# Scores of two head pairs at once on 64x64 tiles, and q and k side by side in 64 rows each

## The chip, the cores and the metric

The kernel runs on one core of a Trainium2 chip. TensorE (PE) multiplies matrices, VectorE (DVE), ScalarE (ACT) and GpSimd (POOL) work on their results, and DMA queues, issued by POOL and SyncE (SP), move data. The metric is the device time of one execution in microseconds (us); lower is better.

## The reference, cut to what matters

Eight batches of eight heads, 576 positions, 64 numbers a head. Attention in a window of 32 positions to either side, plus 8 global positions that see all and are seen by all; then a two-layer network with softplus over the 4608 tokens.

```python
scores = (1 / sqrt(64)) * q @ k.T                       # B=8, H=8, S=576, D=64
mask = |i - j| <= 32  or  i is global  or  j is global  # 8 global positions
attn = softmax(where(mask, scores, -1e9)) @ v
x = attn.transpose(0, 2, 1, 3).reshape(4608, 512)
h = x @ w_in                                            # 512 -> 2048
out = softplus(h) @ w_out                               # 2048 -> 512
```

## The kernel before

**Units.** A unit is 64 query positions of one batch, all eight heads: 9 units a batch, 72 in all. The heads go in four pairs p; a pair's two heads h lie one above the other in 64 rows each. A unit's keys are 136 columns: 64 + 64 of the window and 8 global ones.

**From q and k to scores.** `load_qk` brings q or k of a batch into `qn` or `kn`: 72 rows, each with 8 successive positions of all heads. `tk` and `tq` (L533, L544) turn them, 16 transposes of 72x64 for a pair of heads; `kev` and `qev` copy the results to `kx` and `qx` (copies show as L448). For batches after the first, `qx` holds each unit's 64 queries of the two heads in separate halves of 128 columns, the rest zero (the zeros are set once, by `blanks_q`), so that one matmul of 128x128 with 136 columns gives both heads' scores (`sc`, L662): four matmuls a unit. For batch 0 the queries lie without zeros, and each head has a matmul of its own on a 64x64 tile (L667). `pick` (L491) multiplies with a 0/1 matrix and so gathers the 8 global rows of k and of q, eight matmuls of 512 columns each; `keep`, `turn`, `fill` and `gev` bring them into `kx` and `qg`.

**From scores to tokens.** `top` (L673, DVE) adds the mask and takes the greatest; `ex` (L694, ACT) the exponentials; `su` (L702 to L704, DVE) sums and their inverse; `no` and `gc` (L710, L714, POOL) multiply. The probabilities are turned by PE (`tp`, L720) or by a DMA (`pt`). `val` makes values for four units: 16 or 8 matmuls on 64x64 tiles for the global rows (L775), then 32 on 128x64 tiles for the windows (L785). The global queries have a chain of their own (`sg`, `mx`, `gexp`, `gsum`, `tg`, `lge`, `ov`, `oz`); L610 is in `gsum`.

**MoE.** Nine tiles of 512 tokens: `first` (L819, 64 matmuls of 512 columns), `soft` (L825, ACT), `second` (L830, 64 matmuls), `oev` and the store.

**The order.** Nothing runs in program order: each piece of work is a job with a cost on its engine, a rank, what it waits for and which buffers it opens, and `_Order.run` walks through them once, before the launch, and lays down the order of each engine. `KINDS` says for each kind of PSUM tile how many of the eight banks it may hold and how many must be left spare; `SLOTS` does the same for SBUF; `SWITCH` is what it counts for a change of TensorE's tile shape (`array`); `ASKS`, `HOLDS` and `COMES` are its model of the fetch of PE's instructions. `OPENING` and `LATER` add to the ranks. `add_scores` puts the scores of a tile's units between the `first` jobs of the tile before; `make_batch` adds the work on a new batch's q and k, behind the exponentials of the tile's last unit.

Of the kernel before, what the change touches and what calls it, by code (L numbers as in the profile page):

```python
# [18 lines left out]
class _Order:  # L19
# [30 lines left out]

    def closed(self, key):
        if key is None:
            return 0
        ends = [u["end"] for u in self.users[key]]
        return None if None in ends else max(ends) + self.HOP

    def room(self, opens):

        t0 = 0
        want = 0  # L60
        spare = 0
        for pool, key in opens:
            cap = self.slots.get(pool) or self.kinds[pool][0]
            was = self.opened[pool]
            if len(was) >= cap:
                t = self.closed(was[-cap])
# [12 lines left out]

    def run(self, free):  # L80
# [16 lines left out]
        while ready:  # L97
            best = None
            for j in ready:
# [8 lines left out]
                for e in j["cost"]:  # L108
                    t = max(t0, free[e])
                    rank = j["rank"]  # L110
                    if e == "PE" and array != 128:
                        rank = 0 if j["array"] == array else rank + 1
# [23 lines left out]
            if e == "PE" and j["array"] != array:  # L136
                array = j["array"]
                t += self.SWITCH
# [34 lines left out]
def kernel(  # L173
# [39 lines left out]
    HALVED = 1  # L213
    TURNED = 16
# [26 lines left out]

    def load_qk(b, which, h0=0, h1=H):
# [3 lines left out]
    Q_PARTS = ((0, 0, 32), (32, G, NQ - 32))  # L246
# [15 lines left out]
    load_qk(0, 1, H // 2, H)  # L262
# [25 lines left out]
    posQ2 = temp([P, QR], FP32, "posQ2")  # L288
    count(posQ2[0:G, :], [[1, QR]], 0, QR)
    count(posQ2[G:P, :], [[1, QR]], 32 * QR, QR)  # L290
    pick_w = const([P, QR, 32], BF16, "pick")
    pick_0 = const([P, QR, 32], BF16, "pick0")
# [7 lines left out]
    qx = [const([P, HP, NJ, 2, G], BF16, f"qx{i}") for i in range(2)]  # L300
# [8 lines left out]
    def blanks_q(i):  # L309
        def edges():  # L310
            nc.gpsimd.memset(kx[i][:, :, 0, 0:WIN].bitcast(I32), 0)
            nc.gpsimd.memset(kx[i][:, :, NH5 - 1, G - WIN:G].bitcast(I32), 0)
            clear(nc.gpsimd, qg[i][:])
        return [edges] + [lambda p=p, h=h: nc.gpsimd.memset(qx[i][h * D:(h + 1) * D, p, :, 1 - h, :].bitcast(I32), 0)
                          for p in range(HP) for h in range(2)]
# [13 lines left out]
    for lo, at, n in Q_PARTS:  # L329
        nc.gpsimd.dma_start(out=qn[at:at + n, :, :],  # L330
                            in_=q[0].rearrange("h (q r) d -> q h (r d)", r=QR)[lo:lo + n])
# [50 lines left out]
    def ones_g(i):  # L382
# [3 lines left out]
        for p in range(1, HP):  # L386
            nc.vector.tensor_copy(gw[i][:, :, p, 0:2 * NG], gw[i][:, :, 0, 0:2 * NG])
# [22 lines left out]
    ST, PEB, PNB, PTB, RB = 10, 5, 8, 12, 2  # L410
# [43 lines left out]
    def add_load(b, which, deps):  # L454
# [8 lines left out]
        if b:  # L463
            T["load", b, which] = [o.add({"POOL": (880, 0)}, lambda e: load_qk(b, which), deps + early, rank=0, moves=4300)]
# [9 lines left out]
    def add_prep(b, gate, rank):  # L474
# [4 lines left out]
        if b < 2:  # L479
            blanks["g"] = [T["edges", 0] if b == 0 else T["blank_q", 1]]  # L480
        XN = (qn, kn)

        def pick(e, w):
# [3 lines left out]
            parts = ((pick_w, 0, NQ),) if b or w else tuple((pick_0, at, n) for lo, at, n in Q_PARTS)  # L487
# [21 lines left out]
        def gev(e):  # L509
            for h in range(2):  # L510
                r = slice(h * D, (h + 1) * D)
                copy(e, qg[i][r, :, h * NG:(h + 1) * NG], PS["gt", b][r, 0, :, 0:NG])
        for n, w in enumerate((1, 0)):
            T["pick", b, n] = o.add({"PE": (460 * (1 if b or w else 2), 530 * (1 if b or w else 2))}, lambda e, w=w: pick(e, w),
# [6 lines left out]
                                    [T["keep", b, n], T.get(("turn", b, n - 1)), T["sel8"]], rank=4,  # L521
# [5 lines left out]
        plain = qx[0][:].rearrange("c p j h q -> c p (j h q)")[:, :, 0:S]  # L527
        for p in range(HP):
# [18 lines left out]

            def kev(e, p=p):
# [7 lines left out]
            def qev(e, z=0, p=p, parts=parts):  # L556
                lo, at, n = parts[z]
                t = PS["tq", b, p, z][:].rearrange("c r (j q) -> c j q r", q=G // QR)
                if b == 0:
                    copy(e, plain[:, p, lo * QR:(lo + n) * QR].rearrange("c (j q r) -> c j q r", q=G // QR, r=QR), t)  # L560
                    return
                for h in range(2):
                    c = slice(h * D, (h + 1) * D)
                    copy(e, qx[i][c, p, :, h, :].rearrange("c j (q r) -> c j q r", r=QR), t[c])
            T["tk", b, p] = o.add(mm(QR, NQ), tk, [T["load", b, 1][b == 0 and p >= HP // 2], *gate], rank=rank, opens=[("tk" if b else "tk0", ("tk", b, p))], array=64)
            T["kev", b, p] = o.add({"ACT": (635, 720), "DVE": (800, 880)}, kev, [T["tk", b, p], *late, *blanks["g"]],
                                   rank=3, uses=[("tk", b, p)])
            for z, (lo, at, n) in enumerate(parts):
                key = ("tq", b, p, z)
                T["tqb" if z else "tq", b, p] = o.add(mm(QR, n), lambda e, z=z, f=tq: f(e, z), [T["load", b, 0][z], *gate], rank=rank + z,  # L570
                                                      opens=[("tq" if b else "tq0", key)], array=64)
                n = QR * n
                T["qevb" if z else "qev", b, p] = o.add({"ACT": act(n), "DVE": (90 + 1.2 * n, 170 + 1.2 * n)} if b == 0 else {"ACT": (1270, 1370), "DVE": (1530, 1600)},
                                                        lambda e, z=z, f=qev: f(e, z), [T["tqb" if z else "tq", b, p], *late], rank=3 + z, uses=[key])

        if b == 0:
            T["pick", 0, 1]["deps"] += [T["tqb", 0, HP - 1], T["make_pick"]]
# [3 lines left out]
    def add_global(b, gate, early):  # L581
# [24 lines left out]
        def gsum(e):  # L606
# [3 lines left out]
            nc.vector.scalar_tensor_tensor(out=rv[i][:, 0:2], in0=selg[:, 0, :], scalar=rv[i][:, 2:3], in1=selg[:, 1, :],  # L610
                                           op0=OP.mult, op1=OP.add)
# [27 lines left out]
        T["gsum", b] = o.add({"DVE": (530, 630)}, gsum, [T["gexp", b], T["select"], T.get(("oz", b - 2))], rank=2)  # L639
# [9 lines left out]
    def add_scores(n, gate, rank):  # L649
# [3 lines left out]
        def sc(e, x):  # L653
            if x == 0:
                PS["st", n] = sb.tile([P, HP, EXT], FP32, tag="st", name="st", bufs=ST)
                PS["nb", n] = sb.tile([P, HP], FP32, tag="nb", name="nb", bufs=ST)
            kf = kx[i][:].rearrange("c p a w -> c p (a w)")
            ps = PS["s", n, x] = psum(("s", n, x), [P, 2, EXT], FP32)
            for y in range(2):
                p = x * 2 + y  # L660
                if b:
                    nc.tensor.matmul(out=ps[:, y, :], lhsT=qx[i][:, p, j, :, :].rearrange("c h q -> c (h q)"),  # L662
                                     rhs=kf[:, p, j * W:j * W + EXT], start=True, stop=True)
                    continue
                for h in range(2):
                    r = slice(h * D, (h + 1) * D)
                    nc.tensor.matmul(out=ps[r, y, :], lhsT=qx[0][:].rearrange("c p j h q -> c p (j h q)")[r, p, j * G:(j + 1) * G],  # L667
                                     rhs=kf[r, p, j * W:j * W + EXT], start=True, stop=True)

        def top(e, x):  # L670
            for y in range(2):
                p = x * 2 + y
                nc.vector.tensor_tensor_reduce(out=PS["st", n][:, p, :], in0=PS["s", n, x][:, y, :], in1=mask[:, j, :],  # L673
                                               scale=-SCALE, scalar=3.0e38, op0=OP.add, op1=OP.min,
                                               accum_out=PS["nb", n][:, p:p + 1])
        for x in range(2):
            ready = [T["kev", b, x * 2 + y] for y in range(2)] + [T["fill", b]]
            ready += [T["qevb" if b == 0 and j > 3 else "qev", b, x * 2 + y] for y in range(2)] + [T["blank_q", 2 - b] if 0 < b < 3 else None]
            T["sc", n, x] = o.add(mm(2 if b else 2, EXT), lambda e, x=x: sc(e, x), ready + gate, rank=rank, array=128 if b else 64,
                                  opens=[("s", ("s", n, x))] + ([("st", ("st", n))] if x == 0 else []))  # L680
            gate = [*gate, T["sc", n, 0]]
            T["top", n, x] = o.add({"DVE": (440, 600)}, lambda e, x=x: top(e, x), [T["sc", n, x], *T["mask", 0]], rank=3 if n < 8 else 4,
                                   uses=[("s", n, x), ("st", n)])
# [61 lines left out]
    def add_values(n4):  # L745
# [13 lines left out]
        def val(e):  # L759
# [9 lines left out]
            for y in range(2):  # L769
                for u, e_, b in spans:  # L770
                    for half in range(2):
                        k = slice(half * G, (half + 1) * G)
                        for c in range(2):
                            r = slice(c * G, (c + 1) * G)
                            nc.tensor.matmul(out=PS["xo", n4, half][r, y, u:e_, :], lhsT=oz[b % 2][k, y, r],  # L775
                                             rhs=PS["R", n4][k, u:e_, r], start=(y == 0 and u == 0), stop=False)
            for half in range(2):
                for y in range(2):
                    p = half * 2 + y
# [266 lines left out]
```

## Time and profile before

| | before |
|---|---|
| median of 3 runs | 372.12 us (370.07 to 372.55) |
| profiled execution | 371.55 us, its span 369.8 us |
| PE / DVE / ACT / POOL busy | 95% / 65% / 75% / 41% |
| scores after batch 0 (L662), 128x128, 136 columns | 252 matmuls |
| transposes of k and q (L533, L544) | 1088 matmuls |
| pick (L491) | 136 matmuls |
| first matmul of the MoE (L819) starts | 34.03 us |
| loads of q and k after batch 0 | 14 DMAs of 576 KB, 12.1 and 14.6 us to landing |

A profile page lists, of one execution, how busy each engine was, the chain of work that ended last followed back to the start, and groups of instructions by source line. The trace behind it answers for stages, single lines and stretches of time. The end of a matmul is modelled, so for PE the differences between starts are safer than the lengths shown.

### The profile page before, as it was taken

What the parts mean: (1) busy time and instruction counts of PE and PEld (TensorE: products, weight loads), DVE (VectorE), ACT (ScalarE), POOL (GpSimd) and SP (SyncE); (2) the same over time, 40 slices, a digit from 0 to 9 for tenths busy, and PEclk for the clock granted to TensorE, in tenths of its full rate; (3) what the DMA queues carried; (4) which work ended last, traced back from release to release, by engine and by line L of the source; (5) the groups of instructions that cost most, each with busy time, mean ns of one, the idle gap of its engine ahead of it and who ended that gap; (6) DMA issues with size and microseconds to landing.
All of it is one profiled execution on the core that took longest, in us unless ns stands there. A gap on an engine that the chain in (4) does not pass through costs nothing.

```text
span 369.8 us, 10736 instructions
## 1 busy us (share of the span) xinstructions
PE 350.3 (95%) x4044; PEld 194.3 (53%) x4044; DVE 239.5 (65%) x1028; ACT 277.2 (75%) x724; POOL 153.4 (41%) x258
## 2 busy tenths in 40 slices
PE   1977999999999999999999999999999999999996
PEld 0744777465545554555455545544554455445444
DVE  5689758996679756975697569755975595163011
ACT  3695898997599759885988598959895986784710
POOL 8988820691038503940295029502840180060000
PEclk9999999999999999999999999999999999999999
DMA  6999993099319981698159916980692022021002
GB/s 95 153 234 188 195 168 61 31 104 176 88 44 144 153 156 45 130 144 166 40 132 122 183 40 139 139 170 31 143 107 76 29 87 59 1 73 58 0 30 85
DMA packets 86164, 38.99 MB, mean 105 GB/s; under 512 B 68064, under 2 KB 79584, under 8 KB 86112
## 3 DMA queue, kind: packets, MB, share of 16 engines
q0 software_dynamic: 53248, 18.37, 46.8%
q1 hardware_dynamic: 32864, 19.94, 23.7%
q8 instruction: 31, 0.51, 0.6%
q14 instruction: 21, 0.17, 0.2%
HBM read 36.71 MB, written 9.44 MB: 125 GB/s over the span
## 4 chain that ended last, share of the span: by engine, by line
PE 68%; DVE 15%; ACT 7%; DMA 4%; issue 3%; POOL 3%; DVEq 0%; POOLq 0%; ACTq 0%
PE h L819 34%; PE o L830 16%; DVE sm L702 6%; PE s L662 4%; PE xo L785 3%; ACT pe L694 2%; PE tq L544 2%; DMA qn<-in_q_dram 2%; DVE rs L704 2%; PE pick L491 2%; DVE rs L703 2%; PE tk L533 2%; DVE osb L448 2%; PE xo L775 1%; ACT L602 1%
## 5 line engine op out<-in xcount | busy, mean ns | idle before, releaser
L710 POOL TENSOR_TENSOR pn<-pe,rs 128x512 bf16<-128x512 f32 x72 | 74.7, 1039 | 169.5 <-DVE rs L704 134.4
L819 PE MATMUL h<-xT,win 128*128 128x512 bf16 (+1 forms) x640 | 138.8, 361 | 0.1
L830 PE MATMUL o<-wout,g 128*128 128x512 bf16 (+1 forms) x592 | 136.2, 374 | 0.0
L825 ACT ACTIVATE g<-h 128x512 bf16<-128x512 f32 (+1 forms) x160 | 86.0, 558 | 41.9 <-PE h L819 40.9
L673 DVE CUSTOM_DVE_ANT_0 st<-s,mask 128x136 f32<-128x136 f32 x288 | 69.8, 295 | 45.3 <-PE s L662 43.8
L694 ACT ACTIVATE pe<-st,nb 128x136 f32<-128x136 f32 x288 | 92.1, 403 | 0.8 <-DVE nb L673 0.7
L819 PEld LDWEIGHTS <-win 128*128 128x128 bf16 x640 | 60.1, 99 | 50.9 <-issue 2.0
L830 PEld LDWEIGHTS <-g 128*128 128x128 bf16 x592 | 55.1, 98 | 57.2 <-issue 3.3
L702 DVE TENSOR_REDUCE sm<-pe 128x4 f32<-128x544 f32 x63 | 44.8, 711 | 10.0 <-ACT pe L694 9.8
L448 DVE COPY osb<-o 128x512 f32<-128x512 f32 (+1 forms) x26 | 17.3, 664 | 28.2 <-PE o L830 28.1
L251 POOL DMA_DIRECT2D vA<-in_v_dram x40 | 34.3, 874 | 0.0
L448 DVE COPY qx<-tq 64x576 bf16<-64x576 bf16 (+2 forms) x35 | 25.5, 728 | 5.6 <-PE tq L544 5.0
L662 PEld LDWEIGHTS <-qx 128*128 128x128 bf16 x252 | 20.5, 98 | 14.2 <-issue 0.3
L662 PE MATMUL s<-kx,qx 128*128 128x136 bf16 x252 | 26.9, 223 | 0.0
L673 DVE DVE_READ_ACCUMULATOR2_ANT nb<- 128x1 f32 x288 | 23.8, 83 | 0.0
L448 ACT CAST xT<-xo 128x512 bf16<-128x512 f32 x19 | 10.9, 590 | 12.1 <-PE xo L785 12.1
L533 PE MATMUL tk<-ident_b,kn 72*64 72x72 bf16 x512 | 13.5, 205 | 6.2 <-DMA kn<-in_k_dram 6.2
L448 ACT COPY kx<-tk 128x32 bf16<-128x32 bf16 (+1 forms) x75 | 18.0, 359 | 1.9 <-PE tk L533 1.8
L704 DVE TENSOR_TENSOR rs<-rs,notg 128x4 f32<-128x4 f32 x72 | 17.7, 246 | 2.5
L448 ACT COPY qx<-tq 64x576 bf16<-64x576 bf16 (+2 forms) x29 | 17.2, 593 | 1.9 <-PE tq L544 1.6
L714 POOL TENSOR_TENSOR gw<-pe,rs 128x32 bf16<-128x32 f32 x72 | 17.2, 238 | 3.0 <-DVE rs L704 1.8
L703 DVE RECIPROCAL rs<-sm 128x4 f32<-128x4 f32 x72 | 12.7, 177 | 6.5
(113 smaller groups left out, 347.5 us busy)
## 6 DMA issues: line engine op xcount, KB each, us to landing
out_dram<-osb SPq DMA_DIRECT2D x35, 256.0 KB, 2.2
vB<-vA SPq DMA_DIRECT2D x16, 256.0 KB, 7.0
kn<-in_k_dram POOLq DMA_DIRECT2D x7, 576.0 KB, 12.1
qn<-in_q_dram POOLq DMA_DIRECT2D x7, 576.0 KB, 14.6
vA<-in_v_dram POOLq DMA_DIRECT2D x24, 128.0 KB, 6.4
win<-in_moe_w_in_dram POOLq DMA_DIRECT2D x2, 1024.0 KB, 15.6
wout<-in_moe_w_out_dram POOLq DMA_DIRECT2D x4, 512.0 KB, 10.7
vA<-in_v_dram POOLq DMA_DIRECT2D x16, 96.0 KB, 5.2
```

What stands on the lines that cost most here:

```text
L251: nc.gpsimd.dma_start(out=vA[b % 2][p0:p0 + hi - lo, t, :].rearrange("p (h d) -> p h d", h=H), in_=SRC[2][b, :, lo:hi, :].rearrange("h s d ...
L448: (nc.scalar.copy if e == "ACT" else nc.vector.tensor_copy)(out, in_)
L533: nc.tensor.transpose(out=ps[h * D:(h + 1) * D, r, :], in_=kn[0:NQ, p * 2 + h, r * D:(r + 1) * D], identity=ident_b[0:NQ, 0:NQ])
L662: nc.tensor.matmul(out=ps[:, y, :], lhsT=qx[i][:, p, j, :, :].rearrange("c h q -> c (h q)"), rhs=kf[:, p, j * W:j * W + EXT], start=True, ...
L673: nc.vector.tensor_tensor_reduce(out=PS["st", n][:, p, :], in0=PS["s", n, x][:, y, :], in1=mask[:, j, :], scale=-SCALE, scalar=3.0e38, op0 ...
L694: nc.scalar.activation(out=pe[:, p, 0:EXT], in_=PS["st", n][:, p, :], func=AF.Exp, bias=PS["nb", n][:, p:p + 1], scale=-1.0, **({"accum_ou ...
L702: nc.vector.reduce_sum(out=sm[:], in_=PS["pe", n][:, :, 0:EXT], axis=AX)
L704: nc.vector.tensor_tensor(out=rs[:], in0=rs[:], in1=notg[:, j:j + 1].to_broadcast([P, HP]), op=OP.mult)
L710: nc.gpsimd.tensor_tensor(out=pn[:].rearrange("c p (a s) -> c p a s", a=2), in0=wide[:, :, :, 0:G], in1=rs[:].unsqueeze(2).unsqueeze(3).to ...
L819: nc.tensor.matmul(out=h[:, :], lhsT=w_in_t[c * P // WC][:, kd, c * P % WC:c * P % WC + P], rhs=PS["xT", m][:, kd, lo:hi], start=(kd == 0) ...
L825: nc.scalar.activation(out=PS["g", m, c][:, lo:hi], in_=PS[key][:, :], func=AF.Softplus)
L830: nc.tensor.matmul(out=PS[key][:, :], lhsT=PS["g", m, kf][:, ns * P:(ns + 1) * P], rhs=w_out_t[kf // 4][:, kf % 4, lo:hi], start=(kf == 0) ...
```

## The change

- **Scores.** `qx` has no zeros any more. A unit's scores are eight matmuls on 64x64 tiles. In pair y = 0 head h has rows and columns h; in pair y = 1 the column half is swapped (`h ^ y`), so that two pairs use all four 64x64 tiles. For batches after the first, three units make one job (a burst), in four PSUM banks, 24 matmuls.
- **What follows from the swap.** `ones_g` and `val` use `c ^ y` likewise; `gsum`'s scalar_tensor_tensor becomes two tensor_scalars. `val` may run its two parts in either order (`flip`), whichever meets the tile shape that PE is in.
- **q and k side by side (batches 1 to 7).** One tile `nq` holds q in rows 64 to 127 and k in rows 0 to 63: 8 successive positions a row for the first 512 positions, one a row for the last 64. Each load is two DMAs (`load_main`, `load_rest`). `tkq` turns both at once on 64x64 tiles, 36 transposes of 64 columns a pair of heads, two pairs a job; `kev2` and `qev2` copy. `pick_both` gathers from q and k together on 64x32 tiles, 16 matmuls of 512 columns and 8 of 128.
- **Batch 0.** Loads in the order k heads 0-3, q heads 0-3, k heads 4-7, q heads 4-7, before k, k and two parts of q by rows. The parts of q go, and with them `tqb` and the second half of q's pick. `pick0` is replaced by `pickb`, made later.
- **Memsets.** The 16 of `blanks_q` on `qx` go.
- **The order.** A job can end in another tile shape than it began (`enters`, `both`); `room` counts several banks of one kind that a job opens. The next batch's work waits for an early `first` job of the tile before (`PREP`) instead of the last exponentials. `ST` 10 to 12, `PTB` 12 to 14; other `KINDS`, `OPENING`, `LATER`.

```diff
-    KINDS = dict(h=(4, 2), o=(3, 1), s=(2, 0), pick=(2, 0), gt=(1, 2), tk=(4, 0), tq=(4, 2), tk0=(1, 0), tq0=(2, 0),
-                 sg=(2, 1), tg=(2, 1), ov=(1, 1), tp=(2, 0), rt=(3, 0), xo=(4, 1))
+    KINDS = dict(h=(4, 0), o=(4, 0), s=(4, 0), pick=(4, 0), gt=(1, 2), tk=(2, 0), tq=(3, 2), tk0=(1, 0), tq0=(2, 0),
+                 sg=(3, 0), tg=(2, 1), ov=(1, 1), tp=(3, 1), rt=(4, 1), xo=(4, 1))
...
-        T["load", b, which] = [o.add({"POOL": (880, 0)}, lambda e: load_qk(b, which), deps + early, rank=0, moves=4300)]
+        T["load", b, which] = [o.add({"POOL": (880, 0)}, lambda e: load_main(b, which), deps + early, rank=0, moves=3900),
+                               o.add({"POOL": (850, 0)}, lambda e: load_rest(b, which), deps + early, rank=0, moves=1000)]
...
+        def pick_both(e):
...
+            for r in range(QR + 4):
+                g = r % 4
+                for w in range(2):
+                    rows = slice((1 - w) * G, (2 - w) * G)
+                    hs = slice(0, H) if r < QR else slice(g * 2, g * 2 + 2)
+                    x = min(r, QR)
+                    nc.tensor.matmul(out=PS["pick", b, w][g * 32:(g + 1) * 32, hs, :], lhsT=pick_b[rows, x, :],
+                                     rhs=nq[rows, hs, x * D:(x + 1) * D], start=(r < 4), stop=(r >= QR))
...
+            def tkq(e, p=p):
...
+                for r in range(QR + 1):
+                    for w, ps in ((1, PS["tk", b, p]), (0, PS["tq", b, p, 0])):
+                        rows = slice((1 - w) * G, (2 - w) * G)
+                        for h in range(2):
+                            nc.tensor.transpose(out=ps[h * D:(h + 1) * D, r, :], in_=nq[rows, p * 2 + h, r * D:(r + 1) * D],
+                                                identity=ident_b[rows, rows])
...
+            def qev2(e, p=p):
+                ps = PS["tq", b, p, 0]
+                copy(e, qx[i][:, p, 0:G * QR].rearrange("c (q r) -> c q r", r=QR), ps[:, 0:QR, :].rearrange("c r q -> c q r"))
+                copy(e, qx[i][:, p, G * QR:], ps[:, QR, :])
...
-            nc.vector.scalar_tensor_tensor(out=rv[i][:, 0:2], in0=selg[:, 0, :], scalar=rv[i][:, 2:3], in1=selg[:, 1, :],
-                                           op0=OP.mult, op1=OP.add)
+            for y in range(2):
+                nc.vector.tensor_scalar(out=rv[i][:, y:y + 1], in0=rv[i][:, 2:3], scalar1=selg[:, 0, y:y + 1],
+                                        scalar2=selg[:, 1, y:y + 1], op0=OP.mult, op1=OP.add)
...
                 for h in range(2):
                     r = slice(h * D, (h + 1) * D)
-                    nc.tensor.matmul(out=ps[r, y, :], lhsT=qx[0][:].rearrange("c p j h q -> c p (j h q)")[r, p, j * G:(j + 1) * G],
-                                     rhs=kf[r, p, j * W:j * W + EXT], start=True, stop=True)
...
+                    for y in range(2):
+                        c = slice((h ^ y) * G, (h ^ y) * G + G)
+                        ps, at = PS["s", u, x * 2 + y]
+                        nc.tensor.matmul(out=ps[c, at, :], lhsT=qx[i][r, x * 2 + y, ju * G:(ju + 1) * G],
+                                         rhs=kf[r, x * 2 + y, ju * W:ju * W + EXT], start=True, stop=True)
...
-            make_batch(nb, [T["ex", us[-1]]], 5)
+            make_batch(nb, [T["ex", us[-1]]] if m == 0 else [T["first", m - 1, PREP]], 5)
```

More of the change, by code (lines that the diff above doesn't have):

```diff
@@ L213 @@
     HALVED = 1
+    PREP = 4
     TURNED = 16
@@ L651, in add_scores, with sc @@
         i = b % 2
[L653 to L656, printed above, removed]
+        def sc(e, xs, units):
             kf = kx[i][:].rearrange("c p a w -> c p (a w)")
[L658 to L663, printed above, removed]
-                    continue
+            slots = [(u, x) for u in units for x in range(2)]
+            for u, x in slots:
+                if x not in xs:
+                    continue
+                if x == 0:
+                    PS["st", u] = sb.tile([P, HP, EXT], FP32, tag="st", name="st", bufs=ST)
+                    PS["nb", u] = sb.tile([P, HP], FP32, tag="nb", name="nb", bufs=ST)
+                where = (u - units[0]) * 2 + x
+                for y in range(2):
+                    key = ("s", units[0], where // 3, y)
+                    if where % 3 == 0:
+                        PS[key] = psum(key, [P, 3, EXT], FP32)
+                    PS["s", u, x * 2 + y] = PS[key], where % 3
+                ju = u % NJ
@@ L768, in val @@
                 PS["xo", n4, half] = psum(("xo", n4, half), [P, 2, 4, G], FP32)
[L769 to L776, printed above, removed]
@@ new lines, in globs @@
+            def globs():
+                for y in range(2):
+                    for u, e_, b in spans:
+                        for half in range(2):
+                            k = slice(half * G, (half + 1) * G)
+                            for c in range(2):
+                                r = slice(c * G, (c + 1) * G)
+                                nc.tensor.matmul(out=PS["xo", n4, half][r, y, u:e_, :], lhsT=oz[b % 2][k, y, r],
+                                                 rhs=PS["R", n4][k, u:e_, (c ^ y) * G:(c ^ y) * G + G],
+                                                 start=(not flip and y == 0 and u == 0), stop=(flip and y == 1 and e_ == 4))
@@ new lines, in windows @@
+            def windows():
+                for half in range(2):
+                    for y in range(2):
+                        p = half * 2 + y
+                        for x in range(4):
+                            b, jx = divmod(n4 * 4 + x, NJ)
+                            vw = vA[b % 2][:, jx // 2, :] if jx % 2 == 0 else vB[b % 2][:, jx // 2, :]
+                            for c in range(2):
+                                r = slice(c * G, (c + 1) * G)
+                                nc.tensor.matmul(out=PS["xo", n4, half][r, y, x, :], lhsT=vw[:, p * P + c * G:p * P + (c + 1) * G],
+                                                 rhs=PS["pt", n4 * 4 + x][:, p, (c ^ y) * G:(c ^ y) * G + G],
+                                                 start=(flip and y == 0 and x == 0), stop=(not flip and y == 1 and x == 3))
```

197 lines of the change are left out of this document (120 added, 77 removed).

## The prediction, made before the changed kernel was run

> **What bounds the kernel now.** I read the page first, then the chain, then a table by stage of one period, then the timeline of TensorE inside that period.
>
> ```profile
> span 369.8 us, 10736 instructions
> PE 350.3 (95%) x4044; PEld 194.3 (53%) x4044; DVE 239.5 (65%) x1028; ACT 277.2 (75%) x724; POOL 153.4 (41%) x258
> PE 68%; DVE 15%; ACT 7%; DMA 4%; issue 3%; POOL 3%; DVEq 0%; POOLq 0%; ACTq 0%
> ```
>
> TensorE is busy 95% of the span and holds 68% of the chain that ended last. A busy share alone doesn't prove a bound, since the ends of matmuls are modelled, so I looked at a period by stage (columns: length, then busy time and count of PE, PEld, DVE, ACT, POOL, granted clock, DMA share, GB/s).
>
> ```profile
> 160.30:176.50 16.20, 16.20 (x105) 8.27 (x104) 9.22 (x69) 10.75 (x19) 1.49 (x2) 1.00 1.21 154
> 176.50:191.10 14.60, 14.26 (x101) 6.70 (x101) 10.51 (x29) 13.83 (x42) 7.95 (x13) 1.00 0.30 80
> 191.10:197.50 6.40, 6.40 (x235) 4.59 (x232) 6.16 (x13) 5.44 (x18) 6.15 (x10) 1.00 0.86 117
> ```
>
> Stage A (first MoE matmul, scores between its matmuls) is 16.20 us of 16.20 PE, with ACT and DVE well below. Stage B (exponentials) is close for both: ACT 13.83 of 14.60, while PE fills with the second MoE matmul. Stage C (values, q and k prepared for the next batch) is full for PE, but DVE has 6.16 of 6.40 too. Together 37.2 us, seven times nearly alike. So PE time taken from A is time; from C it is time if the evictions also shrink; in B it is not.
>
> **What the changed work costs now.** The timeline of PE, start and length in us; I use differences of starts.
>
> ```profile
> 175.21 0.40 PE L662 MATMUL s<-kx,qx 128*128 128x136 bf16 x4
> 175.45 1.03 PE L819 MATMUL h<-xT,win 128*128 128x512 bf16 x4
> ...
> 192.12 0.69 PE L533 MATMUL tk<-ident_b,kn 72*64 72x72 bf16 x32
> 192.64 0.43 PE L544 MATMUL tq<-ident_b,qn 72*64 72x72 bf16 x16
> ...
> 193.26 0.62 PE L491 MATMUL pick<-kn,pick 72*32 72x512 bf16 x8
> 193.70 0.60 PE L491 MATMUL pick<-qn,pick 72*32 72x512 bf16 x8
> 194.24 0.39 PE L830 MATMUL o<-wout,g 128*128 128x512 bf16 x1
> ```
>
> Scores: four matmuls from 175.21 to 175.45, 59 ns each in the single starts; 36 a batch is 2.12 us. Transposes: 32 in 0.52 us, 16.25 ns each; 128 a batch is 2.08. Pick: 0.98, and about 0.10 to enter the other tile shape (the start after the last transpose comes 128 ns later instead of 30): 1.08. A batch has 5.28 us of what the change rewrites.
>
> **What it would cost on 64x64 tiles.** The values job already runs 64x64 tiles, four matmuls at once:
>
> ```profile
> 77.70 0.42 PE L775 MATMUL xo<-R,oz 64*64 64x64 bf16 x16
> 78.05 0.25 PE L785 MATMUL xo<-pt,vA 128*64 128x64 bf16 x4
> ...
> 269.03 0.42 PE L775 MATMUL xo<-R,oz 64*64 64x128 bf16 x16
> 269.38 0.22 PE L785 MATMUL xo<-pt,vB 128*64 128x64 bf16 x2
> ```
>
> At 269.03 sixteen matmuls of 128 columns pass in 0.35 us. Their single starts are 3 to 4 ns apart within four, and 55 ns from four to four once going. At 77.70 (half of them 64 columns, half 192) a four of 64 columns is followed 28 ns later by the next. Entering costs 93 ns (309 from the start of a 216 ns matmul), the first four 27 more, leaving 92 to 100: 0.215 us a visit.
>
> 1. Scores, 3 bursts a batch of 24 matmuls: 6 fours x 58.5 ns (55 x 136/128) + 0.215 = 0.566; x3 = 1.70. Gain 0.42 us. Bounds: gain 1.07 if every burst joins other 64x64 work and pays no visit; loss 0.63 if only two run at once (12 x 58.5 + 0.215, x3 = 2.75).
> 2. Transposes, 144 a batch in 2 jobs: 18 fours x 28 ns + 0.215 = 0.72; x2 = 1.44. Gain 0.64 (the transposes of before sat beside value matmuls of their own tile shape and paid no visit). Bounds: gain 1.07 without visits; loss 0.61 at 15.7 ns each, the pace of the 128x64 value matmuls (two in 31 ns): 2.26 + 0.43 = 2.69. I take 28 because that row has the same rows, columns and length.
> 3. Pick, eight tiles of 64x32: 2 x 216 + 55 + 0.20 = 0.69, gain 0.39. No row shows eight at once; with four at once, as L491 does now, 4 x 216 + 2 x 55 + 0.20 = 1.17, loss 0.09. I take eight, since all four of L775 overlapped.
> 4. Sum 1.45 us a batch, seven batches: **10.2 us**.
>
> One rule speaks against item 1: the Trainium skill, TensorEngine Tiling (Array Packing), section Restrictions and Gotchas, says that different row tiles cannot access one PSUM bank at the same time, and the new scores put both heads of a pair, rows 0 to 63 and 64 to 127, into one bank. By the rule the fours split into twos: 2.75 instead of 1.70 us a batch, 7.4 us less gain. The trace disagrees: the scores of the first batch (L667) already write two heads into one bank, and their single starts come in pairs 1 to 6 ns apart, a pair every 113 ns at half the warm pace.
>
> **Evictions.** The q copies fall from 8 of 64x576 (0.75 us DVE, 0.63 ACT) to 4 of 128x512 plus 4 small ones; k gets one small copy (0.18 to 0.26) more for each pair of heads. From some 9.8 to 8.3 us a batch over two engines (estimate from these rows): half of it relieves the DVE in C by 0.75. With PE giving up about 1.0 there, the two shrink alike, so I charge nothing.
>
> **POOL and DMA.** Each q or k load becomes two: 14 more issues of 0.88 us, 1.76 a batch, behind which the normalising multiplies (1.04 each) queue. They come at the end of C, and POOL is idle for 20.36 us of the next A and B before its first multiply; nothing charged. Without that cover, 7 x 1.76 = 12 us. The 7168 small packets, at 37 ns like the v packets of 128 bytes, over 16 engines are 16.7 us in all, in stretches where the DMA has room. The loads have a period to land (12 to 15 us now). The 16 clearing memsets of 0.33 us leave POOL idle time; no gain.
>
> **Instruction supply.** PE once stops inside a job for no semaphore:
>
> ```profile
> 81.05 0.95 PE L544 MATMUL tq<-ident_b,qn 72*64 72x72 bf16 x47
> 82.89 0.19 PE L544 MATMUL tq<-ident_b,qn 72*64 72x72 bf16 x1 [0.90 <-issue]
> ```
>
> Start to start this is 1.10 us. An instruction packet of 16 KB was fetched from 80.64 on, and 87 matmuls with their weight loads had gone in 1.6 us, 107 instructions a us. Stage C above, 467 in 6.40 us (73 a us), never stops. A second stop of 0.74 lies at 120.24. The change adds 60 matmuls, so 120 instructions, to a batch and makes PE quicker through them. Now 1.84 us in seven batches; I charge **3.5 us** more, 0.5 a batch (bounds 0 and 1.1 a batch).
>
> **Opening.** Two things on DVE's chain go:
>
> ```profile
> 17.20 2.01 PE L491 MATMUL pick<-qn,pick 32*32 32x512 bf16 x16
> 19.14 0.66 PE L667 MATMUL s<-kx,qx 64*64 64x136 bf16 x8
> ...
> 27.21 1.67 DVE L610 SCALAR_TENSOR_TENSOR rv<-selg,rv 128x2 f32<-128x2 f32 x1
> ```
>
> The q pick of batch 0 halves to eight matmuls, 0.98 us like k's; DVE waits 1.28 us for it. L610 takes 0.22 us each later time but 1.67 the first; two tensor_scalars (L597: 0.21) replace it, gain 1.25. Against that, the second half of k now lands third instead of second (about 10.5 us instead of 8.1, estimate from the landings), and with it the pick that all scores wait for; from pick (8.16) to DVE's first score work (13.34) it took 5.2 us, of which the turn queued 1.1 behind transposes on PE and the fill 0.5 behind setup on DVE, so 2.4 later becomes some 0.8 lost. I take 1.0 + 1.25 - 0.8 = **1.5 us** gained (bounds: 4 gained if all the DVE idle before 32 goes, 3 lost if the landing counts in full and nothing is won).
>
> **Sum** against the profiled execution's own 371.55 us (median of the three 372.12): 371.55 - 10.2 + 3.5 - 1.5 = **363.4**. Its own range is 356 (half of the five visits a batch saved, 3.8, and no stops) to 369 (a stop of 1.1 a batch, nothing from the opening).
>
> **Rivals.**
> - *Only A gains* (0.15). Prep's PE time hides behind evictions, or moves into B, where ACT is the bound. For it: DVE 6.16 of 6.40. Against: q copies shrink. Scores 7 x 0.42 and the opening's 1.5: 367.1.
> - *Supply eats the gain* (0.13). Prep and two values jobs are about 512 instructions; at 73 a us C takes 7.0 us instead of 6.4. Less the scores' 0.42 that is +0.2 a batch, +1.3, less 1.5: 371.3. For it: the stops above. Against: bank evictions between the two transpose jobs space them out.
> - *The tiles don't overlap four ways* (0.10), the other side. With the loss ends of 1 to 3 a batch costs 0.63 + 0.61 + 0.09 = 1.33 more, seven 9.3, less 1.5: 379.4. It decides from 65 ns a four on (54 fours + 0.645 + 0.43 + 0.69 = 5.28). For it: sustained runs with new weights for each 64-column matmul exist here only on 128x64 tiles. Against: the 28 and 55 ns.
> - *A floor for each matmul* (0.03). L502, 8 columns on 128x128, never starts faster than every 25 ns. At 25 ns scores are 2.45, transposes 4.03, pick 0.69: +1.89 a batch, 383.3. Against: 3 to 4 ns on tiles. The Trainium skill states such a floor, about 60 cycles a matmul (TensorEngine Tiling (Array Packing), Performance Considerations); the trace agrees on full tiles only.
>
> **Chances and range.** The forecast has 0.59. A measurement here tells about 1% from no change. Faster by over 1% (under 368.4): the forecast nearly whole and two thirds of the first rival, 0.69. Within 1%: the rest of these and most of the supply rival, 0.16. Slower: the two tile rivals and a remainder, 0.15. The low end, 353, is the 356 with the opening's full 4; the high end, 374, covers the supply rival. Above it lie the tile rivals, 0.13; below it some 0.04.
>
> **What would show it.** Right: 64x64 score matmuls in fours 58 ns apart, a burst under 0.6 us; a transpose job of 72 near 0.5 us from first to last start; pick near 0.5; the period down from 37.2 to about 36; L610's first 1.67 gone. Wrong: fours at 65 ns or more; "issue" stops of over 1 us in most batches; C no shorter; or first values later than 31.87.

## The result and the profile after

The changed kernel took 400.03 us (median of 4 runs, 399.0 to 403.14), the kernel before beside it 371.24 (370.07 to 372.55): a ratio of 1.0789, 95% interval 1.0713 to 1.0864. The prediction was 363.4, range 353 to 374. It was wrong, in sign and by 37 us. The profiled execution took 399.43 us, its span 397.7.

The same three lines of the page as shown of before, now of the changed kernel:

```profile
span 397.7 us, 11434 instructions
PE 342.6 (86%) x4345; PEld 180.1 (45%) x4392; DVE 232.1 (58%) x1071; ACT 268.7 (68%) x713; POOL 157.0 (39%) x258
PE 63%; DMA 12%; DVE 9%; issue 7%; POOL 5%; ACT 4%; DVEq 0%; POOLq 0%; ACTq 0%
```

PE's busy time did fall, 350.3 to 342.6, though it issues more. But it now sits idle for 55 us of the span instead of 20, and the chain that ended last holds 12% DMA, before 4%; the largest part of it, 5.3%, is loads of q. DMA was the resource to which the prediction charged nothing.

The waits view of the changed kernel (engine and line, what it waited for, us in total, times, longest) says which DMA:

```profile
POOL nq L258 <- PE tq L598: 21.1, 4, 8.1
PE tq L598 <- DMA nq<-in_q_dram: 18.5, 3, 8.9
```

Transposes wait for a load of q, three times, and loads wait for transposes. Only q's load shows as the DMA. The longest case, on PE's and then on POOL's timeline (start, length in us, instruction, idle before and its releaser):

```profile
136.05 0.22 PE L598 MATMUL tk<-ident_b,nq 64*64 64x64 bf16 x2
145.17 0.26 PE L598 MATMUL tq<-ident_b,nq 64*64 64x64 bf16 x2 [8.90 <-DMA nq<-in_q_dram]
```

```profile
137.74 0.72 POOL L258 DMA_DIRECT2D nq<-in_q_dram  x1
146.55 0.68 POOL L258 DMA_DIRECT2D nq<-in_k_dram  x1 [8.10 <-PE tq L598]
```

The second transpose job of a batch has turned its first rows of k. Its q rows wait for a load that POOL issues 1.7 us after the job began. That load belongs to the *next* batch. Then POOL stands until the job ends, with the load of k next in its queue.

The code says how that came about. `tkq` turns q and k together and is registered as `("tk", b, p)`; for batches after 0 there is no `("tq", b, p)` any more. But a line of `add_load` that the diff does not touch builds the load's waits from `T.get(("t" + "qk"[which] + z, b - 1, p))`. For k this still finds the job. For q it finds nothing, and `get` is silent. So the planner let the next batch's q load go as soon as `pick` was done, and in three batches laid it ahead of the second transpose job of the batch before. The order on the engines was then kept to: the job waited for the load. In the jobs that start at 51.31, 98.85 and 136.05 us one start comes 6.92, 3.05 and 9.09 us later than the usual distance after the one before, 19.06 in all; an undisturbed job takes 0.61 us from its first start to its last.

The stall is not all. `nq` exists once, so the load that came too early wrote over the q that the second job was still to turn. In batches 1, 2 and 3 the scores of heads 4 to 7 are made, for the first 512 positions, with the q of the next batch: by its code the changed kernel also computes something else.

The wait has a second price. By windows of the changed kernel (length; busy time and count of PE, PEld, DVE, ACT, POOL; granted clock, DMA share, GB/s):

```profile
136.05:146.10 10.05, 1.15 (x78) 1.04 (x72) 1.39 (x3) 0.90 (x4) 2.40 (x4) 0.58 1.32 137
146.10:151.40 5.30, 5.08 (x29) 1.75 (x18) 1.61 (x6) 3.68 (x9) 4.11 (x5) 0.51 0.76 105
```

After 9 us with PE idle the granted clock is 0.51 for over 5 us; it had fallen 1.6 us into the stop (1.00 from 136.05 to 137.60, 0.50 from 137.70 to 151.25). In the kernel before it is 1.00 over the same times. Matmuls of the MoE ran at half pace here (427 ns from start to start for 512 columns, otherwise 216); behind the three stops that lost some 1.6, 1.7 and 2.5 us.

What the change meant to do did happen. The units of an undisturbed batch on PE's timeline:

```profile
218.71 0.22 PE L598 MATMUL tk<-ident_b,nq 64*64 64x64 bf16 x2
218.76 0.20 PE L598 MATMUL tk<-ident_b,nq 64*64 64x64 bf16 x2
...
219.31 0.20 PE L598 MATMUL tq<-ident_b,nq 64*64 64x64 bf16 x2
219.44 0.68 PE L521 MATMUL pick<-nq,pickb 64*32 64x512 bf16 x24
...
227.38 0.55 PE L747 MATMUL s<-kx,qx 64*64 64x136 bf16 x24
227.86 1.04 PE L921 MATMUL h<-xT,win 128*128 128x512 bf16 x4
```

A job of 72 transposes goes from 218.71 to past 219.31, the pick follows 0.73 us after its start, and a burst of 24 score matmuls gives way to the MoE after 0.48 us.

One more stop is at the very end of the changed kernel:

```profile
389.48 5.83 SPq L939 DMA_DIRECT2D out_dram<-osb  x5
391.66 0.69 DVE L476 COPY osb<-o 128x512 f32<-128x512 f32 x1 [2.21 <-DMA out_dram<-osb]
394.52 0.42 DVE L476 COPY osb<-o 128x256 f32<-128x256 f32 x1 [2.17 <-DMA out_dram<-osb]
```

The last matmul starts at 390.7 and the span ends at 397.7, 7.0 us later; before it was 3.5 (366.3 to 369.8). Several accumulations of the last MoE tile end together, so that copies wait for stores to free `osb`.

### The profile page after: what moved, and what is told of

Same layout as the page of the kernel before. It is cut to its first block, busy times and chain, and to the rows that moved or that the text cites. A ratio compares the mean times of both kernels' runs of the same rounds, so it can differ in the third digit from the quotient of the medians.

```text
span 397.7 us, 11434 instructions
## 1 busy us (share of the span) xinstructions
PE 342.6 (86%) x4345; PEld 180.1 (45%) x4392; DVE 232.1 (58%) x1071; ACT 268.7 (68%) x713; POOL 157.0 (39%) x258
## 4 chain that ended last, share of the span: by engine, by line
PE 63%; DMA 12%; DVE 9%; issue 7%; POOL 5%; ACT 4%; DVEq 0%; POOLq 0%; ACTq 0%
PE h L921 30%; PE o L932 20%; DMA nq<-in_q_dram 5%; DMA win<-in_moe_w_in_dram 4%; DVE sm L794 3%; PE s L747 3%; POOL vA L273 2%; DMA out_dram<-osb 2%; PE xo L883 2%; DVE osb L476 1%; DVE rs L796 1%; ACT L674 1%; PE xo L870 1%; PE tk L598 1%; PE tq L598 1%
## 5 line engine op out<-in xcount | busy, mean ns | idle before, releaser
L932 PE MATMUL o<-wout,g 128*128 128x512 bf16 (+1 forms) x566 | 132.2, 375 | 2.0 <-issue 1.1
L753 DVE CUSTOM_DVE_ANT_0 st<-s,mask 128x136 f32<-128x136 f32 x288 | 65.7, 295 | 44.2 <-PE s L747 44.1
L921 PEld LDWEIGHTS <-win 128*128 128x128 bf16 x640 | 62.5, 102 | 62.1 <-issue 7.0
L794 DVE TENSOR_REDUCE sm<-pe 128x4 f32<-128x544 f32 x63 | 44.6, 709 | 10.3 <-ACT pe L786 10.3
L476 DVE COPY osb<-o 128x512 f32<-128x512 f32 (+1 forms) x30 | 20.3, 677 | 33.8 <-PE o L932 29.4
L476 ACT COPY kx<-tk 128x32 bf16<-128x32 bf16 (+2 forms) x68 | 14.5, 300 | 26.7 <-PE tk L598 15.3
L598 PE MATMUL tq<-ident_b,nq 64*64 64x64 bf16 x504 | 12.5, 202 | 19.9 <-DMA nq<-in_q_dram 18.5
L476 DVE COPY kx<-tk 128x32 bf16<-128x32 bf16 (+2 forms) x56 | 12.8, 292 | 27.9 <-PE tq L598 27.6
L598 PEld LDWEIGHTS <-nq 64*64 64x64 bf16 x1008 | 10.9, 113 | 24.1 <-DMA nq<-in_q_dram 18.8
L747 PE MATMUL s<-kx,qx 64*64 64x136 bf16 x576 | 16.2, 235 | 2.5 <-issue 1.6
L747 PEld LDWEIGHTS <-qx 64*64 64x64 bf16 x576 | 10.2, 111 | 14.2 <-issue 11.9
```

The source lines that it names most:

```text
L476: (nc.scalar.copy if e == "ACT" else nc.vector.tensor_copy)(out, in_)
L598: nc.tensor.transpose(out=ps[h * D:(h + 1) * D, r, :], in_=nq[rows, p * 2 + h, r * D:(r + 1) * D], identity=ident_b[rows, rows])
L747: nc.tensor.matmul(out=ps[c, at, :], lhsT=qx[i][r, x * 2 + y, ju * G:(ju + 1) * G], rhs=kf[r, x * 2 + y, ju * W:ju * W + EXT], start=True, ...
L794: nc.vector.reduce_sum(out=sm[:], in_=PS["pe", n][:, :, 0:EXT], axis=AX)
L921: nc.tensor.matmul(out=h[:, :], lhsT=w_in_t[c * P // WC][:, kd, c * P % WC:c * P % WC + P], rhs=PS["xT", m][:, kd, lo:hi], start=(kd == 0) ...
L932: nc.tensor.matmul(out=PS[key][:, :], lhsT=PS["g", m, kf][:, ns * P:(ns + 1) * P], rhs=w_out_t[kf // 4][:, kf % 4, lo:hi], start=(kf == 0) ...
```

## The experiments

**The load behind the transposes.** The changed kernel with the lost wait put back:

```diff
-        early = [T.get(("t" + "qk"[which] + z, b - 1, p)) for p in range(HP) for z in ("", "b")]
+        early = [T.get(("t" + x + z, b - 1, p)) for x in ("k", "qk"[which]) for p in range(HP) for z in ("", "b")]
```

> The changed kernel, with one dependence more in the order: the loads of the next batch's q stand behind both transposes jobs of this batch, as those of k do. In the changed kernel the loads of q for batches 2, 3 and 4 were laid ahead of the second transposes job of batches 1, 2 and 3, which so turned q rows of the batch after it; here each turns its own. Theory A (the early load is the loss): the stops of 6.9, 3.1 and 9.1 us inside that job go, with them 2 to 4 us of matmuls at the slow clock behind each of the two long ones: 373 to 380 us. Theory B (the q and k loads come too late for the earlier preparation anyway: more and smaller packets, one buffer for both): the wait moves to the first transposes job of the next batch, and the time stays over 390. Theory C (instruction supply and visits to the small tile shape eat what was won): the stops go as under A, but the periods without them stay at 37 to 38 us.

Measured: 371.46 us (370.02 to 375.34) against 372.1, ratio 1.001, interval 0.9968 to 1.0052. That is Theory A, a little under its range: one missing dependence cost 28.6 us of 400. 19.1 of them are the three waits and some 5.8 the MoE matmuls at half clock; the remaining 3.7 were not broken down. The mean granted clock rose from 0.961 to 0.989. Theory C's mark shows too: the last four periods, from the first transposes of one batch to those of the next, still take 37.2 to 38.7 us (before 37.2 to 39.4).

**And the tail.** On top of it, the second matmuls of the last tile get rank 3, behind the first ones:

```diff
-    OWN = {}
+    OWN = {key: 3 for key in T if isinstance(key, tuple) and key[0] == "sec" and key[1] == len(TILES) - 1}
```

> e1 with the second matmuls of the last MoE tile put behind its first ones (a rank of 3 added), as they lay before the change; in the changed kernel four accumulations end within 2 us of each other and their copies and stores queue at the end, 6.8 us from the last matmul's start to the end against 3.3 before. Theory: 3 to 3.5 us less than e1. Rival (the stores take as long either way, since the last one decides): no change against e1.

Measured: 368.49 us (366.23 to 373.67), ratio 0.989, interval 0.9853 to 0.9928; 3.0 less than the run above on the same chip. The last matmul starts at 362.9 and the span ends at 366.4, the 3.5 us of before. This kernel is the nearest to what the prediction costed: the change with its waits complete and the tail as before. It is 1.1% faster than the kernel before; 2.2% was forecast (363.4 of 371.55).

**The early preparation.** The same with the next batch's work behind the last exponentials again:

```diff
-            make_batch(nb, [T["ex", us[-1]]] if m == 0 else [T["first", m - 1, PREP]], 5)
+            make_batch(nb, [T["ex", us[-1]]], 5)
```

> e2 with the next batch's preparation gated on the last exponentials again, as before the change, instead of an early first matmul of the tile before. Theory A: the preparation's place isn't the cause, so within 3 us of e2 either way. Theory B: the waits on q and k go only here, and it is 10 us or more faster than e2.

Measured: 371.62 us, ratio 0.9992, interval 0.9946 to 1.0039. `PREP` is no cause of the loss: without it the time is 3.1 us worse than in the run above, just outside the 3 of Theory A, and the two intervals do not meet.

**Two tensor_scalars alone.** In the kernel before, only the instruction of `gsum`:

```diff
-            nc.vector.scalar_tensor_tensor(out=rv[i][:, 0:2], in0=selg[:, 0, :], scalar=rv[i][:, 2:3], in1=selg[:, 1, :],
-                                           op0=OP.mult, op1=OP.add)
+            for y in range(2):
+                nc.vector.tensor_scalar(out=rv[i][:, y:y + 1], in0=rv[i][:, 2:3], scalar1=selg[:, 0, y:y + 1],
+                                        scalar2=selg[:, 1, y:y + 1], op0=OP.mult, op1=OP.add)
```

> The kernel before, with the scalar_tensor_tensor of gsum made two tensor_scalars, nothing else. My prediction's term: the first 1.67 us of L610 becomes 0.42, and 1.2 us of DVE's chain in the opening goes: 0.5 to 1.3 us faster than before. Rival (DVE waits for something else there, or the first tensor_scalar of this form costs as much): no change in the time of the first values, 31.9 us.

Measured: 371.14 us, ratio 0.9984, interval 0.9939 to 1.0029, too wide to tell 1 us from none. In its profile all 16 instructions take 263 to 274 ns, so the first use's 1.67 us is gone, and the first values start at 31.0 us instead of 31.9, the first MoE matmul at 33.1 instead of 34.0.

**The opening.** In the kernel with the tail mended (the second run above), the first values start at 30.6 us, 1.3 earlier than before, as predicted. But the first matmul of the MoE starts at 35.8, 1.8 later than before, and the second values at 42.3 instead of 40.1. POOL's timeline of that kernel, and then PE's:

```profile
31.35 0.80 POOL L980 DMA_DIRECT2D wout<-in_moe_w_out_dram  x1 [0.77 <-DMA win<-in_moe_w_in_dram]
33.62 0.74 POOL L980 DMA_DIRECT2D wout<-in_moe_w_out_dram  x1 [1.47 <-DVE xT L476]
```

```profile
34.69 0.29 PE L845 MATMUL rt<-ident_b,gw 128*128 128x128 bf16 x1 [2.15 <-POOL gw L806]
35.70 0.29 PE L845 MATMUL rt<-ident_b,gw 128*128 128x128 bf16 x1 [0.72 <-POOL gw L806]
35.78 1.06 PE L921 MATMUL h<-xT,win 128*128 128x256 bf16 x4
```

Loads of `wout`, which nothing needs yet, stand in POOL's queue. One waits 0.77 us for a load of `win` to land, the next 1.47 us for what the profile gives as a copy on DVE; `gw` queues behind them, and PE waits 2.15 and 0.72 us for `gw`. The new `OPENING` and `LATER` put `w_out` at -5 and -6. So both kernels were run with it at 3:

```diff
-    OPENING = dict(first=1.5, firsth=1, gc=-3, gsum=4, mask=-2, oev=4.5, pt=2.5, sec=7.5, softh=4, top=2.5, w_out=-5)
+    OPENING = dict(first=1.5, firsth=1, gc=-3, gsum=4, mask=-2, oev=4.5, pt=2.5, sec=7.5, softh=4, top=2.5, w_out=3)
...
-        pick=4, re=2.5, sc=-1.5, sec=-1, second=-4, su=2.5, tp=-2, w_out=-6)
+        pick=4, re=2.5, sc=-1.5, sec=-1, second=-4, su=2.5, tp=-2, w_out=3)
```

> e2 with the four loads of the second weights (L980, POOL) ranked behind the multiplies of the first eight units (w_out +3 instead of -5 and -6). In e2 two of these issues wait 0.77 and 1.47 us, one of them for the first weights to land, POOL's gw multiplies wait behind them, PE's rt waits 2.41 and 0.96 us for gw, and the first MoE matmul starts at 35.8 us, the second values job at 42.3 (before: 34.0 and 40.1). Theory: the opening's loss is this queue: first MoE matmul by 33.5, second values by 38, and 2 to 4 us less than e2. Rival (the opening is bound by exponentials and their sums): second values stay after 41 and the time stays within 1 us of e2; or the weights come late for the second matmuls (58.9 in e2) and the gain is given back there.

Measured: 364.91 us (362.98 to 367.4), ratio 0.9802, interval 0.9743 to 0.986; 3.6 less than with the tail alone mended. The first MoE matmul starts at 33.2 us, the second values at 37.2, as the theory said. As a control the same in the kernel before (`w_out` from -4 to 3 in both tables):

> The kernel before, with only the four loads of the second weights ranked later, as in e6. A control: if the queue on POOL costs the kernel before as much as it cost e2, the second values job comes before 38 us (40.1 now) and the time falls by 2 to 4 us (364 to 368 of 370 in the span's terms); then that part of e6's gain isn't the change's. Rival: here the issues wait for less, POOL's multiplies are late by under 1.5 us, and the time stays within 1 us.

Measured: 370.32 us, ratio 0.9971, interval 0.9941 to 1.0001: there the queue costs 1 us by the medians, and the interval includes none; the second values still come at 39.4 us. Beside it the mended kernel again:

> e6 once more beside e9 on one chip, in more rounds: 0.975 to 0.985 of the time before. What e6 has over e9 is what the change itself is worth once its queue and its end are mended: 4 us if the steady part gives what e2's trace shows, under 2 if the opening made most of it.

Measured: 365.72 us (362.63 to 368.07), ratio 0.9817, interval 0.9774 to 0.9861. It beats the kernel before by 1.8% and the changed one by about 9% (the ratios divided), and the kernel before with the same later loads by 4.6 us. Its opening on PE's timeline:

```profile
33.00 0.62 PE L845 MATMUL rt<-ident_b,gw 128*128 128x128 bf16 x4
33.43 0.77 PE L921 MATMUL h<-xT,win 128*128 128x256 bf16 x4
```

No wait for `gw`; the second values start at 35.7 us, 4.4 earlier than before.

**What a visit costs.** The kernel with the tail mended, with a burst for each unit instead of every three, nine visits to the 64x64 shape a batch instead of three (the planner's count of instructions in a burst, `MANY`, goes from 48 to 16 with it):

```diff
-        units = [n] if b == 0 else [n - j % 3 + u for u in range(3)]
-        if b == 0 or j % 3 == 0:
+        units = [n]
+        if True:
```

> e2 with a burst of scores for each unit instead of one for three: nine visits to the 64x64 shape a batch instead of three, the same matmuls. Price of a visit by e2's trace: 93 ns in, and 152 ns from the last score to the next matmul where a four takes 58, about 0.19 to 0.22 us. Theory: 6 x 0.2 x 7 = 8 to 9 us more than e2, so above the kernel before (374 to 378). Rival (visits hide beside other waits, or the spread-out scores relieve the instruction supply): under 4 us more.

Measured: 376.54 us (374.97 to 378.68), ratio 1.0114, interval 1.0059 to 1.0169: by the two ratios 8.3 us more than with a burst for three units, over 42 further visits 0.2 us each (0.14 to 0.26 by the intervals, if the order laid down anew costs nothing else).

**Instruction supply.** The kernel before with every transpose of k and q of batches 1 to 7 done twice, 896 more (the same edit in `tk` and `tq`):

```diff
-                for r in range(QR):
+                for r in [r for r in range(QR) for z2 in range(2 if b else 1)]:
```

> The kernel before, every transpose of k and q of batches 1 to 7 done twice in place, the same order else. It adds 128 matmuls, 256 instructions, to a batch. If array time alone counts: 128 x 16.25 ns = 2.08 us a batch, 14.6 in all, 385 to 387 us. If the supply of instructions bounds such stretches at 73 to 90 a us (my charge in the prediction): the 256 take 2.8 to 3.5 us, with stops of 0.5 to 2 us inside the transposes of most batches, 389 to 396 us.

Measured: 419.08 us (416.93 to 421.03), ratio 1.1266, interval 1.1191 to 1.1341: 46 us more, where 896 at 16.25 ns are 14.6. Neither theory went that far. The waits view of this kernel ("issue": the engine waited for nothing that the profile shows):

```profile
PE tq L544 <- issue: 10.3, 6, 2.6
```

Six stops inside transposes of q alone are 10.3 us, where the kernel before has one of 0.90; with those in other lines they come to 19.1, 18.2 more than before. The granted clock falls to half in six stretches; the longest, and the sum of all six (columns as above):

```profile
307.95:318.19 10.24, 9.25 (x145) 5.19 (x138) 4.25 (x8) 4.75 (x10) 0.81 (x2) 0.50 1.41 62
sum 30.71, PE 28.70 PEld 14.46 DVE 10.71 ACT 17.73 POOL 8.82; mean PE 4.78 PEld 2.41 DVE 1.78 ACT 2.96 POOL 1.47
```

PE is busy for 28.70 us of them, so half pace costs some 14 (estimate from this sum). The extra array time, the stops and the half pace come to 14.6 + 18.2 + 14 = 47, which accounts for the 46.

The traces also show with what the "issue" stops go. Each one of over 0.3 us inside a job ends 2.2 to 3.3 us after the start of an instruction packet of 16 KB: the one of the kernel before, four with the tail mended, six in the best kernel, eleven here (after 41 us). So they go with the fetch of PE's instructions: the 1792 instructions that this kernel adds (896 transposes, each with its weight load) bring seven packets more, 38 instead of 31, 256 to a packet. Most packets bring no stop; which ones do is not shown.

In the best kernel the same kind of stop is there. From its PE timeline:

```profile
48.98 0.22 PE L598 MATMUL tq<-ident_b,nq 64*64 64x64 bf16 x2 [2.30 <-issue]
230.78 0.48 PE L747 MATMUL s<-kx,qx 64*64 64x136 bf16 x17 [1.76 <-issue]
```

Inside jobs it stops seven times for "issue", together 8.9 us beyond the usual distance of two starts. In the kernel with the tail mended it is four times, 4.4 us; in the kernel before once, 1.1. The second line shows that a score burst stops too. To see whether smaller jobs avoid it, each batch's transposes were split into four jobs of 36 (`MANY` from 144 to 72):

```diff
-                T["tk", b, p] = T["tk", b, p - 1] if p % 2 else o.add(
-                    {"PE": (500, 650)}, lambda e, f=tkq, p=p: (f(e, p), f(e, p + 1)), [*T["load", b, 1], *T["load", b, 0], *gate, *late], rank=rank, array=65,
-                    opens=[x for y in range(2) for x in (("tk", ("tk", b, p + y)), ("tq", ("tq", b, p + y, 0)))])
+                T["tk", b, p] = o.add(
+                    {"PE": (300, 450)}, lambda e, f=tkq, p=p: f(e, p), [*T["load", b, 1], *T["load", b, 0], *gate, *late], rank=rank, array=65,
+                    opens=[x for y in range(1) for x in (("tk", ("tk", b, p + y)), ("tq", ("tq", b, p + y, 0)))])
```

> The mended kernel with the later w_out loads (365.7 us), but each batch's 144 transposes in four jobs of 36 instead of two of 72. Cost known: two more visits to the 64x64 shape a batch, 0.2 us each, 14 in all, 2.8 us. Theory A (the stops inside the transposes come because a dense job runs ahead of the fetch of PE's instructions): a job of 72 instructions ends before the store is empty, other matmuls stand between, and the five stops inside L598 (2.47 at 46.49, 1.05, 0.99, 1.11 us and the like, 5.6 in all) go: -5.6 + 2.8, about 363. Rival B (the number of instructions in a stretch decides, not where the dense ones stand): the stops stay in sum, within the jobs or behind them, and the visits come on top: about 368.5. Rival C: nothing to see, the order that is laid down anew moves the time by more than either: then the sum of the stops inside jobs of one line tells, 8.9 us in all lines now.

Measured: 398.19 us (396.95 to 400.22), ratio 1.0734, interval 1.0675 to 1.0792. Rival C, and much larger than thought. The order that the planner laid down anew brings the work on two batches together, and values wait for probabilities that a DMA turns:

```profile
140.24 0.26 PE L883 MATMUL xo<-pt,vA 128*64 128x64 bf16 x2 [8.18 <-DMA pt<-pn]
146.77 0.27 PE L883 MATMUL xo<-pt,vB 128*64 128x64 bf16 x2 [6.27 <-DMA pt<-pn]
```

One of those DMAs, issued at 135.99 just behind four loads of `nq`, takes 10.74 us in the chain. From 114.2 to 151.8 us the granted clock is 0.50 as well. The stops inside dense jobs still sum to 7.4 us: 3.4 in picks, 1.5 in transposes, 2.5 in scores. They moved more than they went, which is rival B's mark; but with an order so different the run does not settle which jobs stop.

## Why the prediction was wrong, point by point

- **POOL and DMA: the step that failed.** It said that the loads "come at the end of C" and "have a period to land". That was read off the trace of before and taken as a property of the loads. It is a property of their waits, and the change took one away by a name. I followed each edit in the diff, and not the unedited lines that look the edited names up. Putting the wait back is worth 28.6 us (371.46 after 400.03), more than the whole forecast. Charged was nothing; 19.1 us of PE were lost waiting for loads of q.
- **The tail: no step at all.** New ranks for `sec` and `first` were in the diff; the 3.5 us between the last matmul and the end was never set against them. 3.0 us.
- **Opening: wrong sign, and the part that came true is partly luck.** First values at 30.6 instead of 31.87 is the predicted gain (1.3 of 1.5). But with the tail mended the pick that all scores wait for starts at 11.96 us instead of 8.16, and DVE's first score work at 16.42 instead of 13.34: 3.1 later, where 0.8 was charged. What won that back was not broken down; the two tensor_scalars alone gave 0.9 of the 1.25. What followed the first values was not priced: POOL's queue, with `w_out` moved from rank -4 to -5 and -6. Second values came 2.2 late instead of 1.5 early. With that mended, 4.4 early, above the bound of 4.
- **Scores: right.** 0.093 to enter and 0.482 to the next matmul make 0.575 a burst; 0.566 was predicted. Fours start 58 ns apart. Two tiles of different rows (row tiles) in one PSUM bank did not split them; the Trainium skill's rule (TensorEngine Tiling (Array Packing), Restrictions and Gotchas) would have split each four into two steps, twice the 58 ns; the trace disagrees.
- **Transposes: under-sized.** 34 ns a four, not 28: 0.85 us a job for 0.72. The row at 77.70, from which 28 came, mixes 64 and 192 columns; a run of 64 columns alone is slower. 1.8 us over seven batches.
- **Pick: near.** Eight tiles of 64x32 do overlap: 0.10 to enter and 0.61 to the next matmul, 0.71 where 0.69 was predicted. The floor of 25 ns a matmul (that rival) was nowhere.
- **Sum of the units.** 3 x 0.575 + 2 x 0.85 + 0.71 = 4.14 us a batch instead of 5.28: 1.14 gained, 8.0 over seven, for 10.2. The period was to fall to about 36 us. With the tail mended the last four take 149.1 us together instead of 151.2, 0.5 less each, where 1.45 less 0.5 for the supply was forecast.
- **Instruction supply: right in kind, and its rival was nearer than its 0.13.** The prediction took 1.84 us for before, but its second stop, at 120.24, is no such stop; the waits view gives its idle time to a DMA (`PE xo L785 <- DMA pt<-pn: 0.5, 1, 0.5`). That leaves 1.1. With the tail mended it is 4.4, so 3.3 more, for 3.5 charged. In the best kernel it is 7.8 more: there supply does eat nearly all of the 8.0, and the opening brings 4.4 of the 5.7 us by which its span is shorter (369.8 to 364.1).
- **Does it add up?** Not quite. For the kernel with the tail mended: -8.0 for the units, +3.3 for supply, +2.2 for the opening, and +1.6 for a stretch at half clock that the kernel before does not have (0.50 from 119.90 to 123.25), make -0.9, against a span that is 3.4 shorter; 2.5 are unexplained.

Of the rivals, none named what happened. Each of them asked what PE does on a smaller tile; none asked what the planner does with a changed table of jobs. The slow side had been given 0.15, all of it to tiles.

## What to carry to other kernels

When a change merges or renames jobs in a hand-kept table, look up every line that finds them by name, changed or not, and ask of each lookup what a miss does; a silent miss removes a wait and turns up as another engine's stall, or as data written over before it was read. An order that the engines keep to turns one load laid ahead of the wrong job into a 9 us stop, so the price of an order is read from the trace after, one queue at a time (PE, POOL, SP), and not from the edited lines. Price the visit, the last store and the first load as terms of their own: at 0.2 us a visit, 3 us a tail and 2 to 4 us an opening they were as large here as the array time won.

## What the runs showed of the hardware that was not expected

- Short matmuls in dense runs cost far more than their array time: 896 more transposes (14.6 us) made 46 us, with "issue" stops of 0.5 to 2.6 us inside jobs, each ending 2.2 to 3.3 us after the start of an instruction packet of 16 KB, and 30.7 us at half clock.
- Stops of 3 to 9 us left PE at half clock behind them: granted 0.51 for 5.3 us after the 9.09 us stop. With the tail mended the clock also fell to half for the 3.35 us from 119.90, where the longest stop of PE in the 6 us before was 0.64.
- A first scalar_tensor_tensor took 1.67 us and each later one 0.22; tensor_scalar takes 0.27 every time, the first included.
